# Five tiles of six with the gate in two products: channel 128 written into PSUM ahead of the cosine product

## The chip, the cores and the metric

The kernel runs on one core of one Trainium2 chip. The metric is the device time of one execution in microseconds, the median of the runs. PE is the matrix engine (TensorE), PEld its weight loads, DVE the vector engine, ACT the scalar engine, POOL GpSimd, SP the engine that only issues DMAs.

## The reference

Two parts follow each other: a Fourier mixing of x (8 batches of 3008 rows of 256 channels), and a gated feed-forward layer on the rows that come out of it.

```python
X = np.fft.fft(x, axis=1)
X = np.fft.fft(X, axis=2)
x = X.real.reshape(24064, 256)
gate = np.maximum(x @ w_gate, 0.0)      # w_gate, w_val: 256 x 1536
val = x @ w_val
out = gate * val @ w_out                # w_out: 1536 x 256
```

## The kernel before, in words

**Symmetry.** The real part of the two transforms is a cosine part minus a sine part over the channels. The transform over the channels is multiplied into the weights at the start (WA for the cosine part, WB for the sine part), so that the layer works on U and V, the sequence transforms of folded channels. Two output rows that mirror each other have the same cosine product and opposite sine products. One row set is U·WA + V·WB, the other U·WA - V·WB. V's row 0 would be empty and carries channel 128 instead, whose sign is not turned in the mirrored rows; so WM, the matrix that turns the first set into the second, is -2·WB with row 0 at zero.

**Tiles.** A tile is one slice of 128 hidden units (12 slices, `fi`) by one block of columns. Batch 0 has four blocks (`segments`, 376 or 377 columns), batches 1 to 7 have three (`thirds`, 504, 504 and 497 columns): 36 tiles a batch. A tile gives h for both row sets (`half_h`), in bf16, and 12 tiles of a block are then multiplied with w_out in `out_steps` while the next block's tiles are made.

**An old tile** makes six products: two into g (lines 541 and 542), ACT's relu into SBUF (556), then WM onto the same g (546) and a second relu; likewise two into v, the multiplication with the first relu on DVE (564), WM onto v, and the second multiplication.

**A split tile** (`pair_of_tiles`, 631) has the gate in two products in banks of their own: sine gq (637) and cosine gp (638). ACT copies gq to SBUF as q (641). The sum gp + q is DVE's (647), one input from PSUM. For the difference, ACT has written -2·b2·c for channel 128 into qm (`ch128_part`, 629; c is a row that all partitions hold, CB), POOL adds q (642), DVE subtracts qm from gp (657). Both signs then go through `relu_mult` (568), which reads the gate from SBUF and v from PSUM. v takes three products, as before.

**Order.** The schedule is by hand: every engine runs its instructions in the order in which the program makes them. Tiles go in pairs, one split and one old. Between their steps lie output products (`run(todo_out, ...)`, four at a time), steps of the next batch's DFT (`todo_dft`, numbers per pair in line 739), one eviction or sum at a time (`run_one`), and on POOL the folds and gathers for the batch after the next (`run_fold`, with a credit in us per pair, 2.2 in batch 1 and 1.75 after). The folds (`fold_steps`, 132) are made in batches 1 to 5 and read two SBUF inputs each; the gathers are indirect DMAs that POOL issues (95).

**PSUM** has eight banks: g and v two each (psG), o two (psO, output products), d0 and d1 one each (psD, the two halves of a DFT family, 379). The DFT's odd half is copied to SBUF by ACT (364), and DVE makes sum and difference with the even half from PSUM (367). SBUF scratch of 512 columns comes from `space()`, eight buffers.

Of the kernel before, what the change touches and what calls it, by code (L numbers as in the profile page):

```python
# [32 lines left out]
def kernel(  # L33
# [20 lines left out]
    psG = ctx.enter_context(tc.tile_pool(name="psG", bufs=2, space=PS))  # L54
# [13 lines left out]
    wr = [[single(f"wr{i}{c}", [128, 2, 512], BF16) for c in range(3)] for i in range(2)]  # L68
# [224 lines left out]
    for s in weights(0, (psG, "g", "v"), nc.scalar):  # L293
        s()
# [38 lines left out]
    hp = ctx.enter_context(tc.tile_pool(name="hp", bufs=2 * NF + 2, space=SB))  # L333
# [26 lines left out]
    def combine(st, dst, fam, p, now=True):  # L360
        n = NE if fam == 0 else NJ
        pe, po = st[1], st[0]
        es = rp.tile([128, NE], F32, name="es", tag="es", bufs=2)
        evict.insert(0, lambda: nc.scalar.copy(es[p, 0:n], pe[p, 0:n]))
        for d, op in zip(half_of(dst, fam), (ALU.add, ALU.subtract)):
            m = d.shape[-1]
            sums.append(lambda d=d, op=op, m=m: nc.vector.tensor_tensor(d[p], es[p, 0:m], po[p, 0:m], op=op))  # L367
        if now:
            flush()

    def family(b, dst, fam, sine, pool=None, tags=("d0", "d1")):

        n, cols = (NE, slice(0, NE)) if fam == 0 else (NJ, slice(NE, NK))
        src, tab = (GG[b % 2], tabS) if sine else (FF[b % 2], tabC)
        st = {}

        def mm(par, t, nyq=False):
            if par not in st:
                st[par] = (pool or psD).tile([128, 512], F32, name="d", tag=tags[par])
            rows = slice(0, ROWS[par][t])  # L380
            if nyq:
                nc.tensor.matmul(st[par][0:1, 0:n], lhsT=FF[b % 2][rows, fam, t, par, 128:129], rhs=tabC[rows, 2 * t + par, cols],
                                 start=False, stop=(t == 2), skip_group_check=True)
            else:
                nc.tensor.matmul(st[par][:, 0:n], lhsT=src[rows, 1 - fam if sine else fam, t, par, 0:128],  # L385
                                 rhs=tab[rows, 2 * t + par, cols], start=(t == 0), stop=(t == 2))
        return mm, lambda now=True: combine(st, dst, fam, slice(0, 128), now)

    def dft_first(U, V):

        parts = [(family(0, U, 1, False), 1), (family(0, V, 1, True, psO, ("o", "o")), 2)]
        for t in range(3):
            for (mm, fin), kinds in parts:
                for nyq in range(kinds):
                    for par in (1, 0):
                        mm(par, t, nyq)
                if t == 2:
                    fin()

    def dft_steps(b, U, V, fams, nyq=False, now=False):  # L400
        steps = []
        for fam in fams:
            for dst, sine in ((V, True), (U, False)):
                mm, fin = family(b, dst, fam, sine)
                part = [lambda par=par, t=t, mm=mm: mm(par, t) for par in (1, 0) for t in range(3)]
                if sine and nyq:
                    part.append(lambda mm=mm: [mm(par, t, True) for par in (1, 0) for t in range(3)])
                part[-1] = lambda last=part[-1], fin=fin: (last(), fin(now))
                steps += part
        return steps  # L410

    def nyquist_steps(g, N):

        def one(fam):
            n, cols = (NE, slice(0, NE)) if fam == 0 else (NJ, slice(NE, NK))
            if not paired:
                flush()
            d = psD.tile([128, 512], F32, name="d", tag="d1")
            for k in range(6):
                t, par = k // 2, k % 2  # L420
                rows = slice(0, ROWS[par][t])
                nc.tensor.matmul(d[0:4, 0:n], lhsT=FN[rows, fam, t, par, g].rearrange("p s b -> p (s b)"),  # L422
                                 rhs=tabC[rows, 2 * t + par, cols], start=(k == 0), stop=(k == 5))
            evict.insert(0, lambda: nc.scalar.copy(N[0:4, fam, 0:n], d[0:4, 0:n]))
        return [lambda: one(1), lambda: one(0)]
# [80 lines left out]
    def gate_128():  # L506
        p = psD.tile([128, 512], F32, name="d", tag="d0")
        for f in range(NF):
            nc.tensor.matmul(p[:, f:f + 1], lhsT=WB[0][0:1, f * 128:(f + 1) * 128], rhs=one[:], start=True, stop=True)
        nc.vector.tensor_scalar(b2[:], p[:, 0:NF], scalar1=-2.0, op0=ALU.mult, scalar2=None)  # L510
    more[(2, 2)] = [gate_128]

    DFT_0 = (0, 0, 0, 0, 3, 0, 0, 0, 4, 3, 3, 0), (0,) * 6 + (1,) * 6, (2, 3, 3, 3, 3, 3, 3, 0, 0, 0, 0, 0)
    todo_out, todo_dft, todo_fold = [], [], []
# [33 lines left out]
    def bank(tag):  # L548
        return psG.tile([128, 512], F32, name=tag, tag=tag)

    def space():
        return rp.tile([128, 512], F32, name="r", tag="r", bufs=8)
# [9 lines left out]
    def mult(st, sign):  # L562
        n = st["n"]
        nc.vector.tensor_tensor(half_h(st, sign), st["r"][:, 0:n], st["v"][:, 0:n], op=ALU.mult)  # L564

    def relu_mult(st, sign):
        n = st["n"]
        nc.vector.scalar_tensor_tensor(half_h(st, sign), in0=st["s"][sign][:, 0:n], scalar=0.0, in1=st["v"][:, 0:n],  # L568
# [10 lines left out]
    def gate(st):  # L579
        st["g"] = bank("g")  # L580
        two(st["g"], st, 0)
        relu(st)
# [10 lines left out]
    def single_tile(st, outs, extra=()):  # L593

        gate(st)
# [12 lines left out]
    def first_tile(st, extra):  # L608

        third = st["fi"] % 3 == 2  # L610
        st["g"] = psD.tile([128, 512], F32, name="d", tag="d1") if third else bank("g")
# [5 lines left out]
        st["v"] = psD.tile([128, 512], F32, name="d", tag="d0") if third else bank("v")  # L617
# [8 lines left out]
    def ch128_part(s):  # L626

        s["qm"] = space()
        nc.scalar.activation(s["qm"][:, 0:s["n"]], s["c"], ACTF.Copy, scale=b2[:, s["fi"]:s["fi"] + 1])  # L629

    def pair_of_tiles(s, st, outs, fold_us, ahead):
# [3 lines left out]
        n = s["n"]  # L635
        gq, gp = bank("g"), bank("g")
        nc.tensor.matmul(gq[:, 0:n], lhsT=WB[0][:, s["f"]], rhs=s["vs"], start=True, stop=True)  # L637
        nc.tensor.matmul(gp[:, 0:n], lhsT=WA[0][:, s["f"]], rhs=s["us"], start=True, stop=True)  # L638
        qm = s["qm"]
        q, sp = space(), space()  # L640
        nc.scalar.copy(q[:, 0:n], gq[:, 0:n])  # L641
        nc.gpsimd.tensor_tensor(qm[:, 0:n], qm[:, 0:n], q[:, 0:n], op=ALU.add)  # L642
        run_fold(fold_us)
        if pending is not None:
            finish(pending)
        s["s"] = (sp, qm)
        nc.vector.tensor_tensor(sp[:, 0:n], gp[:, 0:n], q[:, 0:n], op=ALU.add)  # L647
        run(todo_out, outs)
        gate(st)
        if ahead is not None:  # L650
            ch128_part(ahead)
        run_one(evict)
        value(st)
        mult(st, 0)
        run(todo_out, outs)
        value(s)
        nc.vector.tensor_tensor(qm[:, 0:n], gp[:, 0:n], qm[:, 0:n], op=ALU.subtract)  # L657
        relu_mult(s, 0)
        mirror(st["g"], st, 0)
        relu(st)  # L660
        run_one(evict)
        run(todo_out, outs)
        finish(st)
        run_one(sums)
        run(todo_out, outs)
        return s

    ahead = None

    for b in range(B):  # L670
# [4 lines left out]
        for blk, block in enumerate(blocks):  # L675
# [9 lines left out]
            if blk == (0 if b else 2) and b + 1 < B:  # L685
                Un, Vn = new_uv()
                todo_dft = dft_steps(b + 1, Un, Vn, (1, 0), now=not b)
                CBn = up.tile([128, 4 * NJ + 2], BF16, name="CB", tag="CB")
                steps, todo_dft = todo_dft, []
# [27 lines left out]
            elif not paired:  # L717
                for fi in range(NF):
                    st = tile_of(block, fi, (U, V, CB))
                    add_h(st, hs)  # L720
                    if (blk, fi) == (3, 11):
                        ahead = tile_of(thirds[0], 0, (Un, Vn, CBn))
                        more[(blk, fi)] = [lambda: ch128_part(ahead)]
                    pending = single_tile(st, per_tile // 2, more_b.get((blk, fi), ()))
                    run(todo_dft, DFT_0[blk - 1][fi])
            else:
                for fi in range(0, NF, 2):
                    at = 6 * blk + fi // 2
                    s, st = ahead, tile_of(block, fi + 1, (U, V, CB))
                    for tile_ in (s, st):  # L730
                        add_h(tile_, hs)
                    if fi + 2 < NF:
                        ahead = tile_of(block, fi + 2, (U, V, CB))
                    elif blk < 2:
                        ahead = tile_of(blocks[blk + 1], 0, (U, V, CB))
                    else:
                        ahead = tile_of(blocks[0], 0, (Un, Vn, CBn)) if b + 1 < B else None
                    pending = pair_of_tiles(s, st, per_tile // 2, 2.2 if b == 1 else 1.75, ahead)
                    run(todo_dft, (2, 1, 3)[at % 3] if at < 9 else (1, 1, 2, 1, 3)[at - 9] if at < 14 and b % 2 else (2, 1, 3, 0, 0)[at - 9] if at < 14 else 0)
# [39 lines left out]
```

## Time and profile before

| what | us |
|---|---|
| median of 3 runs | 670.19 (670.15 to 670.19) |
| the profiled execution | 670.19 |
| its span | 668.4 |
| PE busy | 645.5 |
| DVE busy | 564.9 |
| ACT busy | 426.5 |
| POOL busy | 404.0 |

The span is the time from the first to the last instruction in the profile; the execution's own time lies around it. A matmul's mean duration is longer than the distance to the next, since matmuls are pipelined: the chain of waits shows what each of them holds up. A row of a group shows the line, engine, operation, tiles and shapes, then the busy time and the mean of one, then the idle time of the engine just before these instructions with what ended it. In the timeline the columns are start, duration, engine, line and operation; a bracket gives the idle time before and who ended it.

### The profile page before, as it was taken

To read this page: it belongs to the slowest core of one execution; us is meant where nothing else is said; L and a number is where in the kernel's file an instruction comes from. 1 tells how busy PE (TensorE), PEld (TensorE's weight loads), DVE (VectorE), ACT (ScalarE), POOL (GpSimd) and SP (SyncE) were. 2 spreads that over 40 slices of the span, in tenths; PEclk is the share of its full clock that TensorE was granted. 3 is DMA by queue.
4 is the path that set the end of the run, shared out by engine and by line. 5 is a ranking of instruction groups with operands and counts; after the bars stand their busy time and mean duration, and the time that the engine had idled before them with its cause. 6 is when DMAs were issued, how large, how long until landed. Compare 5 with 4: busy or idle time off the path is not lost.

```text
span 668.4 us, 12335 instructions
## 1 busy us (share of the span) xinstructions
PE 645.5 (97%) x4266; PEld 413.6 (62%) x4266; DVE 564.9 (85%) x988; ACT 426.5 (64%) x798; POOL 404.0 (60%) x485
## 2 busy tenths in 40 slices
PE   0999999999999999999999999999999999999997
PEld 0456676665666666665666666666666666666666
DVE  8876566998988999898898989889898999999991
ACT  8796566666665666665666656656665666666662
POOL 7589996886777675775667657676622222233330
PEclk9999999999999999999999999999999999999999
DMA  8922653242324133142322422211121112111112
GB/s 223 196 65 63 193 154 111 71 132 62 102 77 123 47 104 86 38 139 64 89 76 54 133 86 78 78 31 34 46 71 31 42 38 70 33 52 42 46 48 78
DMA packets 42439, 55.26 MB, mean 83 GB/s; under 512 B 5153, under 2 KB 32353, under 8 KB 42376
## 3 DMA queue, kind: packets, MB, share of 16 engines
q1 hardware_dynamic: 34552, 39.23, 19.4%
q0 software_dynamic: 7536, 14.72, 9.1%
q8 instruction: 33, 0.54, 0.4%
q10 hardware_dynamic: 288, 0.52, 0.2%
q14 instruction: 30, 0.25, 0.1%
HBM read 32.14 MB, written 24.67 MB: 85 GB/s over the span
## 4 chain that ended last, share of the span: by engine, by line
PE 93%; DVE 4%; ACT 2%; issue 1%; DMA 0%; SPq 0%; POOL 0%; DVEq 0%; ACTq 0%; POOLq 0%
PE o L470 37%; PE v L546 9%; PE v L541 9%; PE v L542 9%; PE g L546 5%; PE g L541 5%; PE g L542 5%; PE d L385 4%; PE g L637 4%; PE g L638 4%; PE d L422 1%; ACT r L556 1%; DVE PQ L114 1%; DVE m L226 1%; DVE XG L106 1%
## 5 line engine op out<-in xcount | busy, mean ns | idle before, releaser
L470 PE MATMUL o<-wo,h 128*128 128x256 bf16 x2304 | 345.6, 273 | 0.0
L470 PEld LDWEIGHTS <-h 128*128 128x128 bf16 x2304 | 225.4, 98 | 123.9 <-issue 1.7
L642 POOL TENSOR_TENSOR r<-r 128x504 f32<-128x504 f32 (+1 forms) x126 | 157.6, 1250 | 227.3 <-ACT r L641 227.2
L556 ACT ACTIVATE r<-g 128x504 f32<-128x504 f32 (+3 forms) x340 | 191.2, 565 | 135.8 <-PE g L542 102.3
L564 DVE TENSOR_TENSOR h<-r,v 128x504 bf16<-128x504 f32 (+3 forms) x340 | 214.6, 640 | 53.1 <-ACT r L556 33.3
L568 DVE SCALAR_TENSOR_TENSOR h<-r,v 128x504 bf16<-128x504 f32 (+1 forms) x252 | 169.4, 672 | 27.6 <-PE v L546 23.7
L641 ACT COPY r<-g 128x504 f32<-128x504 f32 (+1 forms) x126 | 72.8, 578 | 82.8 <-PE g L637 82.8
L546 PE MATMUL v<-V,WM 128*128 128x504 bf16 (+3 forms) x296 | 108.6, 367 | 0.3
L541 PE MATMUL v<-U,WA 128*128 128x504 bf16 (+3 forms) x296 | 108.7, 367 | 0.1
L542 PE MATMUL v<-V,WB 128*128 128x504 bf16 (+3 forms) x296 | 108.7, 367 | 0.0
L629 ACT ACTIVATE r<-CB,b 128x504 f32<-128x504 bf16 (+1 forms) x126 | 88.8, 705 | 0.0
L647 DVE TENSOR_TENSOR r<-g,r 128x504 f32<-128x504 f32 (+1 forms) x126 | 84.9, 674 | 0.0
L657 DVE TENSOR_TENSOR r<-g,r 128x504 f32<-128x504 f32 (+1 forms) x126 | 84.9, 674 | 0.0
L546 PEld LDWEIGHTS <-WM 128*128 128x128 bf16 x474 | 46.2, 98 | 35.0 <-issue 0.5
L476 ACT COPY os<-o 128x512 f32<-128x512 f32 x96 | 55.8, 581 | 10.6 <-PE o L470 8.5
L541 PEld LDWEIGHTS <-WA 128*128 128x128 bf16 x474 | 46.3, 98 | 26.1 <-issue 3.5
L546 PE MATMUL g<-V,WM 128*128 128x504 bf16 (+3 forms) x170 | 61.4, 361 | 0.7 <-ACT r L556 0.5
L542 PE MATMUL g<-V,WB 128*128 128x504 bf16 (+3 forms) x170 | 61.4, 361 | 0.5 <-DVE V L367 0.5
L541 PE MATMUL g<-U,WA 128*128 128x504 bf16 (+3 forms) x170 | 61.5, 362 | 0.4 <-DVE U L367 0.3
L542 PEld LDWEIGHTS <-WB 128*128 128x128 bf16 x474 | 46.3, 98 | 23.7 <-ACT WB L284 0.7
L95 POOL DMA_INDIRECT XG<-in_x_dram,gidx x48 | 48.8, 1017 | 8.8 <-issue 5.4
L106 POOL TENSOR_TENSOR XG<-XG,XD 128x510 f32<-128x510 f32 x42 | 52.3, 1266 | 0.1
(108 smaller groups left out, 494.5 us busy)
## 6 DMA issues: line engine op xcount, KB each, us to landing
out_dram<-os SPq DMA_DIRECT2D x118, 128.0 KB
XD<-in_x_dram SPq DMA_DIRECT2D x30, 256.0 KB
out_dram<-os SPq DMA_DIRECT2D x62, 120.0 KB
XD<-in_x_dram SPq DMA_DIRECT2D x16, 240.0 KB
CB<-ch SPq DMA_DIRECT2D x7, 376.2 KB
out_dram<-os SPq DMA_DIRECT2D x10, 127.0 KB
XG<-in_x_dram,gidx POOLq DMA_INDIRECT x48, 3.9
wr<-in_moe_w_gate_dram POOLq DMA_DIRECT2D x3, 256.0 KB, 7.3
```

The source lines that it names most:

```text
L470: nc.tensor.matmul(st["p"][:, q, :], lhsT=hs[f][:, sign, h0:h0 + 128], rhs=wo[:, f, :], start=(f == 0), stop=(f == NF - 1))
L541: nc.tensor.matmul(bank[:, 0:st["n"]], lhsT=WA[i][:, st["f"]], rhs=st["us"], start=True, stop=False)
L542: nc.tensor.matmul(bank[:, 0:st["n"]], lhsT=WB[i][:, st["f"]], rhs=st["vs"], start=False, stop=True)
L546: nc.tensor.matmul(bank[:, 0:st["n"]], lhsT=WM[i][:, st["f"]], rhs=st["vs"], start=False, stop=True, skip_group_check=True)
L556: nc.scalar.activation(st["r"][:, 0:st["n"]], st["g"][:, 0:st["n"]], ACTF.Relu)
L564: nc.vector.tensor_tensor(half_h(st, sign), st["r"][:, 0:n], st["v"][:, 0:n], op=ALU.mult)
L568: nc.vector.scalar_tensor_tensor(half_h(st, sign), in0=st["s"][sign][:, 0:n], scalar=0.0, in1=st["v"][:, 0:n], op0=ALU.max, op1=ALU.mult)
L629: nc.scalar.activation(s["qm"][:, 0:s["n"]], s["c"], ACTF.Copy, scale=b2[:, s["fi"]:s["fi"] + 1])
L641: nc.scalar.copy(q[:, 0:n], gq[:, 0:n])
L642: nc.gpsimd.tensor_tensor(qm[:, 0:n], qm[:, 0:n], q[:, 0:n], op=ALU.add)
L647: nc.vector.tensor_tensor(sp[:, 0:n], gp[:, 0:n], q[:, 0:n], op=ALU.add)
L657: nc.vector.tensor_tensor(qm[:, 0:n], gp[:, 0:n], qm[:, 0:n], op=ALU.subtract)
```

## The change

Instead of pairs there is one loop over tiles, `slot(cur, nxt, after)`, with the kinds "nnnnno": five split tiles, then an old one. In a slot the gate of the next tile is made and the value of the current one.

For a split tile the steps are: `seed`, one slot ahead, in which ACT writes b2·c (now with the factor 1) into the PSUM bank of the cosine part; `sine_part`, one product into g, with WM, which holds no channel 128, copied by ACT to SBUF as q with the factor -0.5; `cosine_part`, one product onto the seeded bank, which ACT copies to SBUF, and POOL's difference copy - q; and `plus`, DVE's sum copy + q, both inputs from SBUF. An old tile's gate keeps its three products on g, all in the slot ahead of its value.

The PSUM banks are dealt out anew: g one, p (cosine part) two, v two, o two, d one. The DFT's halves therefore go one behind the other through d, with an eviction between them (`end(par)`), and the steps per slot are DFT_EVEN and DFT_ODD. `space()` has twelve buffers; the weights' raw tiles share the pool of h. The folds' credit is 1.1 per slot in batch 1 and 0.9 after. Batch 0 takes other banks for the same steps, and its last tile primes the two p banks with a product each and makes the first split gate.

```diff
-    psG = ctx.enter_context(tc.tile_pool(name="psG", bufs=2, space=PS))
+    psG = ctx.enter_context(tc.tile_pool(name="psG", bufs=1, space=PS))
+    psP = ctx.enter_context(tc.tile_pool(name="psP", bufs=2, space=PS))
+    psV = ctx.enter_context(tc.tile_pool(name="psV", bufs=2, space=PS))
...
-        nc.vector.tensor_scalar(b2[:], p[:, 0:NF], scalar1=-2.0, op0=ALU.mult, scalar2=None)
+        nc.vector.tensor_scalar(b2[:], p[:, 0:NF], scalar1=1.0, op0=ALU.mult, scalar2=None)
...
+    DFT_EVEN = (3, 0, 3, 0, 0, 0) * 4 + (0,) * 12
+    DFT_ODD = (3, 0, 3, 0, 0, 0) * 3 + (1, 0, 1, 0, 3, 0, 3) + (0,) * 11
...
-        return rp.tile([128, 512], F32, name="r", tag="r", bufs=8)
+        return rp.tile([128, 512], F32, name="r", tag="r", bufs=12)
...
+    KINDS = "nnnnno"
...
+    def prime():
+        p = bank("p")
+        nc.tensor.matmul(p[:], lhsT=WA[0][:, 0:128], rhs=U[:, 0:512], start=True, stop=True)
+        return p
+
+    def seed(st, p=None):
+        if st is None or st["kind"] == "o":
+            return
+        st["p"] = p or bank("p")
+        nc.scalar.activation(st["p"][:, 0:st["n"]], st["c"], ACTF.Copy, scale=b2[:, st["fi"]:st["fi"] + 1])
+
+    def sine_part(st):
+        n = st["n"]
+        st["g"] = bank("g")
+        nc.tensor.matmul(st["g"][:, 0:n], lhsT=WM[0][:, st["f"]], rhs=st["vs"], start=True, stop=True)
+        st["q"] = space()
+        nc.scalar.activation(st["q"][:, 0:n], st["g"][:, 0:n], ACTF.Copy, scale=-0.5)
+
+    def cosine_part(st):
+        n = st["n"]
+        nc.tensor.matmul(st["p"][:, 0:n], lhsT=WA[0][:, st["f"]], rhs=st["us"], start=False, stop=True, skip_group_check=True)
+        st["s"] = copy, sp, sm = [space() for _ in range(3)]
+        nc.scalar.copy(copy[:, 0:n], st["p"][:, 0:n])
+        nc.gpsimd.tensor_tensor(sm[:, 0:n], copy[:, 0:n], st["q"][:, 0:n], op=ALU.subtract)
+
+    def plus(st):
+        n, (copy, sp, _) = st["n"], st["s"]
+        nc.vector.tensor_tensor(sp[:, 0:n], copy[:, 0:n], st["q"][:, 0:n], op=ALU.add)
+
+    def slot(cur, nxt, after, outs, fold_us):
+        stop = len(todo_out)
+        def out(part):
+            run(todo_out, len(todo_out) - stop + outs * part // 8)
+        old = nxt is not None and nxt["kind"] == "o"
+        new = nxt is not None and not old
+        if old:
+            gate(nxt)
+        elif new and cur["kind"] != "o":
+            sine_part(nxt)
+        out(3)
+        if new:
+            if cur["kind"] == "o":
+                sine_part(nxt)
+                out(5)
+            cosine_part(nxt)
 +        run_fold(fold_us)
+        seed(after)
+        out(5)
+        finish(pending)
+        value(cur)
+        if cur["kind"] == "o":
+            mult(cur, 0, cur["first"])
+        else:
+            relu_mult(cur, 0)
+        if new:
+            plus(nxt)
+        run_one(evict)
+        run_one(sums)
+        out(6)
+        if old:
+            nxt["first"] = nxt["r"]
+            mirror(nxt["g"], nxt, 0)
+            relu(nxt)
+        out(8)
+        return cur
...
+                    pending = slot(cur, *ahead, per_tile, 1.1 if b == 1 else .9)
+                    run(todo_dft, DFT_ODD[at] if b % 2 else DFT_EVEN[at])
```

## The prediction

> **What bounds the kernel now.** I read the page's busy times first, then the busy times by stretch, with the span after the first batch cut into the seven equal parts that batches 1 to 7 take (the first product of line 637 starts at 111.2, the last batch's tiles end at 653.6: 77.5 us each).
>
> ```profile
> PE 645.5 (97%) x4266; PEld 413.6 (62%) x4266; DVE 564.9 (85%) x988; ACT 426.5 (64%) x798; POOL 404.0 (60%) x485
> ```
>
> ```profile
> 111.20:188.70 77.50, 77.36 (x499) 47.97 (x497) 68.78 (x116) 49.29 (x90) 59.21 (x67) 1.00 0.31 90
> 188.70:266.20 77.50, 77.50 (x515) 50.11 (x513) 69.94 (x118) 49.02 (x88) 53.59 (x62) 1.00 0.31 89
> 266.20:343.70 77.50, 77.50 (x509) 49.10 (x508) 68.16 (x114) 48.14 (x88) 51.20 (x60) 1.00 0.29 84
> 343.70:421.10 77.40, 77.40 (x514) 50.04 (x513) 69.83 (x117) 49.19 (x90) 52.72 (x62) 1.00 0.30 86
> 421.10:498.60 77.50, 77.50 (x511) 49.28 (x509) 68.16 (x114) 48.50 (x89) 46.49 (x56) 1.00 0.15 47
> 498.60:576.10 77.50, 77.50 (x513) 50.04 (x512) 70.09 (x117) 49.06 (x89) 22.50 (x18) 1.00 0.16 46
> ```
>
> Columns after the length: PE, weight loads, DVE, ACT, POOL, granted clock, DMA. The reader is to see that PE has no hole in these batches and the full clock, so every product taken away is time, as long as nothing else becomes late; and that POOL is a different engine in batches 1 to 4 (folds of later batches) than in 6 and 7. In the chain of waits a 504-column product takes 0.21 us (three in 0.635: 0.2115), four output products 0.44 (0.109 each). Twelve thirds of a batch are 36 tiles, so a tile lasts 2.15 us.
>
> **What goes from PE.** A batch has 18 split tiles (5 products) and 18 old ones (6); after it, 30 and 6. So 12 x 7 = 84 products go: 84 x 0.2115 = **-17.8 us**, 2.54 per batch. The DFT and output products stay.
>
> **What is added on each engine.** These are the prices that the page gives:
>
> ```profile
> L642 POOL TENSOR_TENSOR r<-r 128x504 f32<-128x504 f32 (+1 forms) x126 | 157.6, 1250 | 227.3 <-ACT r L641 227.2
> ...
> L641 ACT COPY r<-g 128x504 f32<-128x504 f32 (+1 forms) x126 | 72.8, 578 | 82.8 <-PE g L637 82.8
> ...
> L629 ACT ACTIVATE r<-CB,b 128x504 f32<-128x504 bf16 (+1 forms) x126 | 88.8, 705 | 0.0
> L647 DVE TENSOR_TENSOR r<-g,r 128x504 f32<-128x504 f32 (+1 forms) x126 | 84.9, 674 | 0.0
> ```
>
> and this stretch of the timeline gives what they take one behind the other:
>
> ```profile
> 303.47 0.71 ACT L629 ACTIVATE r<-CB,b 128x504 f32<-128x504 bf16 x1
> 303.58 1.09 POOL L114 TENSOR_TENSOR PQ<-XG 128x510 f32<-128x510 f32 x1
> ...
> 303.60 0.68 DVE L564 TENSOR_TENSOR h<-r,v 128x504 bf16<-128x504 f32 x1 [0.16 <-ACT r L556]
> ...
> 304.02 0.38 PE L546 MATMUL g<-V,WM 128*128 128x504 bf16 x1
> ...
> 304.20 0.68 DVE L657 TENSOR_TENSOR r<-g,r 128x504 f32<-128x504 f32 x1
> ...
> 304.43 0.59 ACT L556 ACTIVATE r<-g 128x504 f32<-128x504 f32 x1 [0.26 <-PE g L546]
> ```
>
> The reader is to see that DVE starts its next operation 0.60 after the last (a stretch later 0.59), not 0.68; ACT likewise 0.49 behind a read of PSUM (300.18 to 300.67) and 0.60 behind L629; and that a product's result is read 0.41 after its start (304.02 to 304.43).
>
> A slot of the changed loop with a split tile behind a split tile has 5 products and 8 output products on PE: 5 x 0.2115 + 8 x 0.109 = 1.93 us, plus its share of the DFT.
> - **DVE**: two relu-multiplies and the add `plus`, 3 x 0.59 = 1.77. The subtraction of L657 goes to POOL. Six slots (five split, one old) come to 5 x 1.77 + 2 x 0.59 + 0.6 for the DFT's sums = 10.6, against PE's 5 x 1.93 + 2.14 + 0.64 = 12.4: it fits.
> - **ACT**: two copies and the seed, 2 x 0.49 + 0.60 = 1.58, with evictions 1.8 of 1.93; six slots about 10.2 of 12.4. The seed writes PSUM from SBUF, which the trace doesn't show; its ends are the copy (0.578) and L629 (0.705); I take L629, the same operation, and the lower end would change nothing, since it is wanted by PE only in the next slot, 0.2 to 0.3 us after it ends.
> - **POOL**: 12 more subtractions per batch at 1.25 = +15.0. With the columns above: 74.2, 68.6, 66.2, 67.7, 61.5, then 37.5 and 38.7 of some 76 us. POOL's subtraction of a tile is wanted two slots later, about 2.5 us after it should be ready, which covers a fold in front of it (up to 1.82).
> - **The DFT** keeps its products; its one bank d is emptied by ACT (0.36) in the slot between the odd and the even half, and by two sums in the slots after, so nobody waits; were that cover gone, each of 8 halves would cost PE up to 0.9 us in a batch.
> - **SP** keeps its DMAs and their order; POOL's gathers stay behind the same fold steps, one tile at a time instead of two.
>
> **A new wait of PE.** psG now has one buffer for g. Of a slot whose next tile is old, the mirrored gate product is the last long one, then come 2 + 3 output products (0.545 us) and then the next tile's sine product, which needs that bank. The relu ends 0.41 + 0.59 after the mirror product's start, and PE takes up ACT's end 0.05 later (40.85 to 40.90 in the trace): 1.05 - 0.2115 - 0.545 = **0.29 us** of PE idle, with all outputs of the slot and the DFT queued behind it. Nothing covers it: the DFT steps lie in other slots (but for one). 42 old tiles x 0.29 = **+12.2 us**. Before, g had two buffers and the trace shows no such wait.
>
> **Start of batch 1**: two priming products (0.43) and a cosine product that waits for its seed (0.41 + 0.71 + 0.05 after the prime, with 0.64 of work before it: about 0.5): **+0.9**. It holds tile 11 of the last segment, once.
>
> **The step that decides: the add's two inputs.** L647 took one input from PSUM. `plus` takes both, the copy and q, from SBUF, 30 times per batch, while POOL's subtractions and folds read two SBUF inputs each. In a slot the copy ends at 1.53 us, POOL's subtraction runs from 1.67 to 2.9, and DVE reaches `plus` at 2.56: they meet in every slot. No row shows such a pair. While POOL folds, every DVE operation of batches 1 to 7 has one input in PSUM; the folds that DVE makes itself run while POOL only issues DMAs, and POOL then waits for them (L309, 7.2 us idle). So the ends are: nothing lost (an add of 510 elements with both inputs in SBUF, L114 on DVE, took 686 ns with POOL issuing DMAs), and full turns, 0.68 us of POOL per add. What is nearest to a meeting is this:
>
> ```profile
> 10.21 0.83 POOL L214 DMA_DIRECT2D wr<-in_moe_w_gate_dram  x1
> 10.60 0.49 DVE L222 TENSOR_SCALAR qd<-dvec,ums 128x129 f32<-128x129 f32 x1
> ...
> 11.66 0.29 DVE L222 TENSOR_SCALAR qd<-dvec,ums 128x129 f32<-128x129 f32 x1
> ```
>
> The same operation on the same shape took 0.49 and 0.29; the long one ended 0.05 behind POOL's instruction. It is one row and another kind of operation, but it is a sign of turns. I take turns, for the time in which the add passes data: 504 x 1.04 ns (L106 against L114 on DVE: 1216 - 686 over 510 elements) = 0.525. Per batch 30 x 0.525 = 15.8, less 3.0 for adds that meet a gather (some 9% of the time) and for POOL's operations overlapping by 0.03. POOL's column becomes 87.0, 81.4, 79.0, 80.5, 74.3. Where it is above PE's 77.5 - 2.54 + 6 x 0.29 = 76.7, DVE waits at `plus`, the relu-multiplies queue behind it, and PE waits for them at its mirror products. Batches 1 to 4: +9.5 + 3.9 + 1.5 + 3.0; batches 5 to 7: -0.8 each; start +0.9. Sum **+16.4**.
>
> The trace can show no more here. The Trainium skill, SBUF — State Buffer, Who interferes with whom, says it outright: a DVE instruction with two SBUF inputs and a GpSimd instruction that reads SBUF exclude each other, and the second to start waits for the whole of the first. It speaks against this change, and no run so far shows it; by it the forecast's sum stands nearer its upper end, by its absence the next case holds.
>
> The profiled execution took 670.19 us, its span 668.4, the rest lies around it; the median of the runs is the same 670.19. So 670.2 + 16.4 = **687 us**. With full turns and nothing taken off, the columns are 94.5, 88.9, 86.5, 88.0, 81.8, the sum +52 and the time 722; with 0.42 per add it is 675. Range of this case 674 to 712.
>
> **Rivals.**
> 1. *Faster: the add and POOL don't disturb each other.* For it: L114's 686 ns, and that six-slot sums of all engines fit. Then -17.8 + 12.2 + 0.9 = -4.7: **665.5** (655 if the wait for g is hidden after all). The point from which it turns: at about 0.34 us of POOL per add batch 1 alone eats the 4.7 us. That is half of the way between the ends, which is why neither case is far ahead.
> 2. *Slower without turns*: POOL in batch 1 has 1.1 us of folds per slot beside 1.25; five split slots take 2.35 each against PE's 2.0, so it falls back 1.7 us in six slots, over its 2.5 of slack with one long fold; and ACT has 0.2 us of slack at the seed. Each 0.04 us in 210 split slots is 8 us: **674**.
> 3. *It comes out even*: a small loss of either kind against the 4.7 us: **670**.
>
> **Chances**: turns 0.50 (687), rival 1 0.36 (665.5), rival 2 0.07, rival 3 0.07. Within 0.2% (1.3 us, about what a measurement of this kernel can tell from no change) is rival 3; slower is 0.57. The range for 8 in 10 must reach to rival 1: 662 to 710.
>
> **What would show it.** Of the changed kernel: 84 fewer 504-column products; PE idle of about 0.3 us before the sine product, released by the relu, 41 times; `plus` at more than 0.68 us, or POOL's subtraction above 1.25 in the slots where both run, in all batches; batches 1 to 4 longer than 77.5 and 6 to 7 about 76.7. If `plus` stays at 0.68 and POOL's rows at 1.25, the decisive step is wrong and the time is rival 1's. If batches 6 and 7 are long as well, another engine than POOL is late.

## The result and the profile after

The changed kernel takes **743.55 us** (median of 4 runs, 742.31 to 744.28) against 670.19: ratio 1.109 [1.107, 1.111], 73 us slower. The forecast was 687, its range ended at 710. The profiled execution took 742.31 us, its span 740.5 (before: 670.19 and 668.4).

The page of the changed kernel, busy times, granted clock and chain of waits by engine:

```profile
PE 655.8 (89%) x4182; PEld 408.7 (55%) x4184; DVE 640.9 (87%) x946; ACT 532.4 (72%) x1008; POOL 550.9 (74%) x569
...
PEclk9999998879999999999989999999999999999999
...
PE 60%; DVE 21%; issue 14%; ACT 3%; POOL 1%; DMA 0%; DVEq 0%; SPq 0%; ACTq 0%; POOLq 0%
```

84 products are gone, and still PE's busy time grew by 10.3 us. Part of that is the clock: in the columns by batch below, PE's busy time times what the granted clock lacked comes to some 15 us in batches 1 to 4. Another part is bookkeeping, since a product with a pause behind it shows its full 0.38 us where the next one used to follow after 0.21. PE is no longer what is always busy. DVE's busy time grew by 76 us (564.9 before), though it makes fewer instructions (946 for 988), and it has 21% of the chain. No engine has its whole span full; that is what a loop of waits between engines looks like.

The costliest groups of the changed kernel (busy, mean ns of one, then idle time before them and who ended it):

```profile
L679 POOL TENSOR_TENSOR r<-r 128x504 f32<-128x504 f32 (+1 forms) x210 | 274.4, 1310 | 150.9 <-ACT r L678 144.7
...
L582 DVE SCALAR_TENSOR_TENSOR h<-r,v 128x504 bf16<-128x504 f32 (+1 forms) x420 | 268.3, 670 | 47.6 <-PE v L560 41.9
L683 DVE TENSOR_TENSOR r<-r 128x504 f32<-128x504 f32 (+1 forms) x210 | 249.0, 1185 | 2.1 <-ACT r L678 2.1
...
L560 PE MATMUL v<-V,WM 128*128 128x504 bf16 (+3 forms) x296 | 110.3, 373 | 55.9 <-DVE h L582 52.9
L665 ACT ACTIVATE p<-CB,b 128x504 f32<-128x504 bf16 (+1 forms) x210 | 145.0, 691 | 0.6 <-PE v L556 0.6
...
L113 POOL TENSOR_TENSOR XG<-XG,XD 128x510 f32<-128x510 f32 x42 | 60.9, 1463 | 0.1
```

Read the second and third numbers. The relu-multiply (L582) has the mean that it had, 670. The add `plus` (L683) has a mean of 1185 where L647 had 674: 210 x 0.51 = 107 us of DVE's time. POOL's fold L113 went from 1266 ns (L106 of before) to 1463. PE stood idle for 55.9 us ahead of its mirror product (L560), and 52.9 of that was ended by the relu-multiply, which stands behind the add on DVE. The seed (L665), a write into PSUM, costs 691 ns, and PE hardly waited for ACT.

All adds in the view of one source line (shortest, median, longest ns):

```profile
L683 DVE TENSOR_TENSOR r<-r x210: 665/874/8695, 113.7 to 721.5; 128x504 f32<-128x504 f32 x70, 128x497 f32<-128x497 f32 x35
```

An undisturbed add still takes 665 ns; half take over 874, and one takes 8695. Thirteen took over 1.9 us and have 43 of the 107 us; three of these (2.30 to 2.33 us) waited for one long fold of 1.8 us, the other ten for two to seven POOL instructions, and those ten have 38 us.

Busy times by batch, 1 to 6, cut at the first sine product of each (the columns of the forecast's table):

```profile
111.40:216.90 105.50, 83.21 (x483) 48.63 (x482) 95.20 (x109) 65.03 (x121) 81.74 (x79) 0.90 0.23 68
216.90:307.10 90.20, 79.56 (x499) 49.23 (x499) 84.22 (x108) 64.40 (x118) 76.41 (x73) 0.98 0.25 73
307.10:398.80 91.70, 82.13 (x511) 50.16 (x511) 82.55 (x111) 64.93 (x120) 76.02 (x74) 0.96 0.24 73
398.80:488.60 89.80, 79.30 (x498) 49.08 (x498) 84.26 (x111) 64.19 (x118) 76.22 (x74) 0.98 0.25 74
488.60:574.10 85.50, 79.55 (x511) 49.30 (x511) 78.64 (x113) 64.78 (x120) 70.48 (x69) 1.00 0.15 46
574.10:650.60 76.50, 75.74 (x498) 48.66 (x498) 69.59 (x110) 63.98 (x118) 37.66 (x30) 1.00 0.15 47
```

Cut in the same way, the batches of before took 77.7, 77.2, 79.5, 77.2, 79.5, 77.2 and 88.7 with the end (odd batches hold the Nyquist products). So the 72 us are +27.9, +13.0, +12.2, +12.7, +6.0, -0.7, +1.2: they lie in the batches with folds on POOL, and batch 6, where POOL only subtracts, is faster than before. And POOL, the last busy column, is idle for 13.8 us of batch 2.

One add that meets one subtraction, in the timeline of batch 3 (start, duration):

```profile
328.77 1.25 POOL L679 TENSOR_TENSOR r<-r 128x504 f32<-128x504 f32 x1
...
329.29 1.28 DVE L683 TENSOR_TENSOR r<-r 128x504 f32<-128x504 f32 x1
...
329.99 1.71 POOL L113 TENSOR_TENSOR XG<-XG,XD 128x510 f32<-128x510 f32 x1
```

POOL's subtraction ends at 330.02, the add at 330.57, 0.55 later; POOL's fold, taken up at 329.99, ends 1.13 behind the add, a little less than its undisturbed length of 1.27. That is a turn: the add waits for all of the subtraction, then the fold waits for the add. The rule weighed in the forecast (the Trainium skill, SBUF — State Buffer, Who interferes with whom: of the two the second waits for the whole of the first) agrees with these three numbers.

The longest add, in batch 1:

```profile
139.88 1.27 POOL L679 TENSOR_TENSOR r<-r 128x504 f32<-128x504 f32 x1
...
140.28 8.70 DVE L683 TENSOR_TENSOR r<-r 128x504 f32<-128x504 f32 x1
...
141.10 1.28 POOL L113 TENSOR_TENSOR XG<-XG,XD 128x510 f32<-128x510 f32 x1
...
142.32 1.25 POOL L679 TENSOR_TENSOR r<-r 128x504 f32<-128x504 f32 x1
...
143.53 2.48 POOL L113 TENSOR_TENSOR XG<-XG,XD 128x510 f32<-128x510 f32 x2
...
145.97 1.24 POOL L679 TENSOR_TENSOR r<-r 128x504 f32<-128x504 f32 x1
147.18 1.25 POOL L113 TENSOR_TENSOR XG<-XG,XD 128x510 f32<-128x510 f32 x1
...
150.66 0.58 PE L560 MATMUL v<-V,WM 128*128 128x504 bf16 x1 [7.76 <-DVE h L582]
```

Here the turn is missed. Seven POOL instructions run one behind the other at their plain lengths, the next taken up as the last ends, and the add ends at 148.98, 0.55 behind the seventh (148.43). PE waits 7.76 us and comes back at a lower clock (its product then takes 0.58 in place of 0.38).

### The profile page after: what moved, and what is told of

It reads as the page before. It is cut to its first block, busy times and chain, and to the rows that moved or that the text cites. A ratio compares the mean times of both kernels' runs of the same rounds, so it can differ in the third digit from the quotient of the medians.

```text
span 740.5 us, 12781 instructions
## 1 busy us (share of the span) xinstructions
PE 655.8 (89%) x4182; PEld 408.7 (55%) x4184; DVE 640.9 (87%) x946; ACT 532.4 (72%) x1008; POOL 550.9 (74%) x569
## 4 chain that ended last, share of the span: by engine, by line
PE 60%; DVE 21%; issue 14%; ACT 3%; POOL 1%; DMA 0%; DVEq 0%; SPq 0%; ACTq 0%; POOLq 0%
PE o L481 22%; DVE h L582 10%; PE v L560 7%; DVE r L683 6%; PE v L556 6%; PE v L555 6%; PE g L670 5%; PE p L676 4%; PE d L383 2%; ACT r L570 2%; DVE h L578 1%; PE d L433 1%; PE g L560 1%; PE p L560 1%; PE p L556 1%
## 5 line engine op out<-in xcount | busy, mean ns | idle before, releaser
L679 POOL TENSOR_TENSOR r<-r 128x504 f32<-128x504 f32 (+1 forms) x210 | 274.4, 1310 | 150.9 <-ACT r L678 144.7
L582 DVE SCALAR_TENSOR_TENSOR h<-r,v 128x504 bf16<-128x504 f32 (+1 forms) x420 | 268.3, 670 | 47.6 <-PE v L560 41.9
L683 DVE TENSOR_TENSOR r<-r 128x504 f32<-128x504 f32 (+1 forms) x210 | 249.0, 1185 | 2.1 <-ACT r L678 2.1
L672 ACT ACTIVATE r<-g 128x504 f32<-128x504 f32 (+1 forms) x210 | 124.1, 591 | 89.1 <-PE g L670 54.2
L560 PE MATMUL v<-V,WM 128*128 128x504 bf16 (+3 forms) x296 | 110.3, 373 | 55.9 <-DVE h L582 52.9
L665 ACT ACTIVATE p<-CB,b 128x504 f32<-128x504 bf16 (+1 forms) x210 | 145.0, 691 | 0.6 <-PE v L556 0.6
L578 DVE TENSOR_TENSOR h<-r,v 128x376 bf16<-128x376 f32 (+3 forms) x172 | 101.0, 605 | 28.3 <-PE v L560 16.9
L678 ACT COPY r<-p 128x504 f32<-128x504 f32 (+1 forms) x210 | 121.5, 579 | 1.5 <-PE p L676 1.1
L570 ACT ACTIVATE r<-g 128x504 f32<-128x504 f32 (+3 forms) x94 | 54.7, 582 | 73.2 <-PE g L560 40.1
L670 PE MATMUL g<-V,WM 128*128 128x504 bf16 (+1 forms) x210 | 80.2, 382 | 4.8 <-ACT r L672 0.2
L676 PE MATMUL p<-U,WA 128*128 128x504 bf16 (+1 forms) x210 | 79.7, 380 | 0.5 <-ACT p L665 0.4
L102 POOL DMA_INDIRECT XG<-in_x_dram,gidx x48 | 56.3, 1172 | 8.7 <-issue 5.7
L113 POOL TENSOR_TENSOR XG<-XG,XD 128x510 f32<-128x510 f32 x42 | 60.9, 1463 | 0.1
```

The costliest lines, as they stand in the source:

```text
L560: nc.tensor.matmul(bank[:, 0:st["n"]], lhsT=WM[i][:, st["f"]], rhs=st["vs"], start=False, stop=True, skip_group_check=True)
L570: nc.scalar.activation(st["r"][:, 0:st["n"]], st["g"][:, 0:st["n"]], ACTF.Relu)
L665: nc.scalar.activation(st["p"][:, 0:st["n"]], st["c"], ACTF.Copy, scale=b2[:, st["fi"]:st["fi"] + 1])
L670: nc.tensor.matmul(st["g"][:, 0:n], lhsT=WM[0][:, st["f"]], rhs=st["vs"], start=True, stop=True)
L672: nc.scalar.activation(st["q"][:, 0:n], st["g"][:, 0:n], ACTF.Copy, scale=-0.5)
L678: nc.scalar.copy(copy[:, 0:n], st["p"][:, 0:n])
```

## The experiments

The theories. **Turns on DVE**: an add with both inputs in SBUF waits for POOL instructions that read SBUF, and what it loses is lost on DVE, where the relu-multiplies stand behind it. Rival A, **POOL's column** (the forecast's own reckoning): the loss counts as POOL's time, so it shows only where POOL is nearly full. Rival B: most of the 73 us is from the new order and the banks, not from the add.

### e1: the sum takes the cosine part from PSUM

```
-        nc.vector.tensor_tensor(sp[:, 0:n], copy[:, 0:n], st["q"][:, 0:n], op=ALU.add)
+        nc.vector.tensor_tensor(sp[:, 0:n], st["p"][:, 0:n], st["q"][:, 0:n], op=ALU.add)
```

> The changed kernel, but the add takes the cosine part from PSUM instead of ScalarE's copy: one input in SBUF, everything else as it is. If the add and POOL take turns because both inputs come from SBUF: the add 0.68 us everywhere (median 0.87, longest 8.7 now), POOL's subtraction 1.25, batches 1 to 5 at 76 to 79 us, time 663 to 669. If POOL's own load (68 to 74 us of work in a batch of 77) or another engine is what is late: adds still wait or others do, and the time stays above 715.

Measured: **670.54 us**, ratio to before 1.0006 [0.9997, 1.0016]. All 73 us are gone; the time is 1.5 us above the range expected for it. The page's busy times and the source line of the add in this kernel:

```profile
PE 637.0 (95%) x4184; PEld 405.0 (61%) x4184; DVE 541.2 (81%) x946; ACT 529.4 (79%) x1008; POOL 507.6 (76%) x569
```

```profile
L683 DVE TENSOR_TENSOR r<-p,r x210: 668/676/683, 114.1 to 649.7; 128x504 f32<-128x504 f32 x70, 128x497 f32<-128x497 f32 x35
```

The same 210 adds now lie between 668 and 683 ns, beside the same subtractions and folds. Against it the changed kernel's DVE is busy 99.7 us longer and POOL 43.3. Rival B falls: every other part of the change is in this kernel. That the sum now waits for the cosine product itself and no longer for ACT's copy doesn't explain the gain, since DVE stood idle for that copy for only 2.1 us in the changed kernel (row L683 above). But e1 is not faster than before, as rival 1 of the forecast had it (665.5): its batches take 79.6, 76.5, 79.0, 76.5, 79.0, 76.5 and 90.1. The even ones gain the 0.7 to 0.8 forecast; batch 1 loses 1.9, and the last with the end 1.4.

This also sizes the loss. By batch the adds of the changed kernel have 30.6, 21.3, 17.0, 19.2, 11.4, 3.9 and 3.9 us over 0.675 each; its batches are longer than those of this kernel by 26.0, 13.7, 12.7, 13.4, 6.5, 0.0 and -0.2. What DVE loses above some 4 to 8 us in a batch is lost to the kernel, although e1's DVE is idle for 10 to 15 us of a batch.

### e2: no folds for batches 3 to 7

```
+        if b > 2:
+            steps = [s if s in gathers or s[0] == 0.0 else (s[0], lambda: None) for s in steps]
```

> The changed kernel without POOL's fold arithmetic for batches 3 to 7 (gathers and loads stay, so the rows of those batches are wrong). If what costs is the meeting of the add with a chain of POOL operations: batches 1 to 5 become like batch 6 (76.5; odd ones 78), adds at 0.67 to 1.04, time 664 to 670. If each meeting costs by itself, with the subtraction alone as well: batches 1 to 5 stay above 82 and the time above 700.

Measured, in one run: **687.46 us**. Folds carry 56 of the 73 us; neither expectation held. The batches take 87.2, 79.7, 81.3, 80.2, 79.0, 76.5. Batch 1 still makes what is left of batch 2's folds, and there are adds like this one, behind a gather (timeline, batch 3; lines are two higher here):

```profile
271.45 1.25 POOL L102 DMA_INDIRECT XG<-in_x_dram,gidx  x1 [0.17 <-issue]
...
272.74 2.44 POOL L681 TENSOR_TENSOR r<-r 128x497 f32<-128x497 f32 x2
272.90 2.81 DVE L685 TENSOR_TENSOR r<-r 128x497 f32<-128x497 f32 x1
```

The gather held up one subtraction, so two run in a row, and the add ends behind both. So what this add lost went by how many reading instructions POOL had in a row when it came; batches 6 and 7, where POOL only subtracts, are as in the changed kernel.

### e5: the kernel before, with only its sum's inputs both in SBUF

```
+        cp = rp.tile([128, 512], F32, name="cp", tag="cp", bufs=1)
+        nc.scalar.copy(cp[:, 0:n], gp[:, 0:n])
...
-        nc.vector.tensor_tensor(sp[:, 0:n], gp[:, 0:n], q[:, 0:n], op=ALU.add)
+        nc.vector.tensor_tensor(sp[:, 0:n], cp[:, 0:n], q[:, 0:n], op=ALU.add)
```

> The kernel before with one thing of the change alone: ScalarE also copies the cosine part to SBUF (126 copies more), and DVE's sum takes both inputs from SBUF. If only POOL's column counts, as the prediction summed it: columns of 69, 63, 61, 62 and 56 us, all below 77.5, and no loss: 670 to 673. If DVE's wait at each meeting counts: DVE is busy 69 of 77.5 and 18 waits of 0.5 us or more a batch do not fit, so batches 1 to 5 grow by 3 us or more: above 685.

Measured: **705.56 us**, ratio 1.0523 [1.0505, 1.0541]. The source line of this sum:

```profile
L649 DVE TENSOR_TENSOR r<-cp,r x126: 892/1352/3647, 113.0 to 686.4; 128x504 f32<-128x504 f32 x84, 128x497 f32<-128x497 f32 x42
```

Not one of 126 sums is below 892 ns (669 to 678 before). The added copies aren't what they wait for: ahead of these sums DVE was idle for ACT's copy once, for 0.2 us. The batches take 87.7, 82.3, 86.0, 84.1, 82.3, 79.8 and 91.3. This settles A: POOL has but 434.8 us of work in a span of 704.7, so its column is far from full, and batch 6, in which POOL was busy for 22.5 of 77.5 us, grows too, by 2.6. Eighteen adds of this form per batch, with their copies, cost the kernel before 35 us, in another order of work and without any other part of the change.

### e7 and e8: what POOL does while the add runs

Both are e2 with POOL's subtraction replaced, so no fold is in the way after batch 1.

e7:

```
-        nc.gpsimd.tensor_tensor(sm[:, 0:n], copy[:, 0:n], st["q"][:, 0:n], op=ALU.subtract)
+        nc.gpsimd.memset(sm[:, 0:n], 0.0)
```

e8:

```
-        nc.gpsimd.tensor_tensor(sm[:, 0:n], copy[:, 0:n], st["q"][:, 0:n], op=ALU.subtract)
+        nc.gpsimd.tensor_copy(sm[:, 0:n], copy[:, 0:n])
```

> As the kernel without the fold arithmetic (687.5), and POOL's subtraction is replaced by writing zeros of the same size (the difference and the folds of batches 3 to 7 are left out, so half of the rows are wrong). If the add and POOL share a way of reading: adds 0.67 to 0.70 even while POOL writes, time 664 to 671. If any POOL instruction holds the add: it is still stretched where the two meet, and the time stays above 680.

> The same, but POOL copies the cosine part instead of subtracting (one input from SBUF; the difference and the folds are left out). If two inputs on both sides are needed for a turn: adds 0.68 and 664 to 671. If one POOL read is enough: adds stretched to as much as the copy's rest plus 0.54, fewer and shorter than with the subtraction, 668 to 682.

Measured, one run each: e7 **668.24 us**, e8 **668.97**. The source lines of e7's add and of its memset, and one meeting in its timeline:

```profile
L685 DVE TENSOR_TENSOR r<-r x210: 669/675/1510, 113.7 to 647.4; 128x504 f32<-128x504 f32 x70, 128x497 f32<-128x497 f32 x35
```

```profile
L681 POOL MEMSET r<- x210: 513/517/521, 108.9 to 643.8; 128x504 f32 x70, 128x497 f32 x35
```

```profile
128.71 0.68 DVE L685 TENSOR_TENSOR r<-r 128x504 f32<-128x504 f32 x1
128.91 0.52 POOL L681 MEMSET r<- 128x504 f32 x1
```

In 125 of the 210 adds of e7 a memset runs for over 0.15 us beside the add, and none of these adds is above 0.72 us; the memset keeps its 0.517. The one of 1510 met a leftover fold. A POOL instruction that only writes SBUF doesn't hold the add, nor does the add hold it. The Trainium skill, SBUF — State Buffer, Who interferes with whom, says so too, and this run agrees. The add of e7 reads two SBUF inputs like that of the changed kernel, so the two inputs alone, without POOL reading beside them, cost nothing.

e8 says less: its time lies in both expected ranges, and the copy of 0.6 us mostly ends before the add comes. In batch 1 six copies began while an add had still 0.4 us or more to go, and all six took 0.87 to 1.12 us where the median is 0.607; the first two began 0.03 us behind the start of an add of 0.683 and ended 0.46 behind its end. So a POOL instruction with one SBUF input waits for the add too; that such a copy holds an add, no case shows cleanly.

### e9: POOL waits for the sum before it folds

```
-        run_fold(fold_us)
...
             plus(nxt)
+            nc.gpsimd.tensor_copy(go[:, 1:2], nxt["s"][1][:, 0:1])
+        run_fold(fold_us)
```

> The changed kernel (sum of two SBUF inputs, all folds), but POOL gets its folds behind the add of the slot, and before them copies one column of the sum, so that it can't start a fold until the add has run. If part of the loss is turns that the add loses to several POOL operations in a row (adds of 2.3 to 8.7 us, some 30 us in all): no add above 1.9, time 705 to 730. If the plain turns are the whole loss: 740 to 750, or more for the added wait.

Measured: **732.95 us**, ratio 1.0932 [1.0913, 1.0950], between the two expectations. The adds in this kernel:

```profile
L683 DVE TENSOR_TENSOR r<-r x210: 665/960/4545, 113.7 to 712.5; 128x504 f32<-128x504 f32 x70, 128x497 f32<-128x497 f32 x35
```

Batch 1 fell from 105.6 to 92.2, the others stayed within 3 us (92.4, 88.8, 89.7, 87.0, 77.4, and 92.9 with the end). The longest wait is halved, the median is up: POOL is later, makes 210 small reads more, and in batches 6 and 7 all 30 adds are above 0.72 us in place of 24 and 21. The expectation of no add above 1.9 us failed: batch 1 has four of them in place of five, batches 2 to 5 ten in place of eight. So e9 made the missed turns of batch 1 shorter and took none away elsewhere. That waits for single POOL instructions cost time by themselves is seen in batch 5 of the changed kernel: no add there took over 1.9 us, and it lost 6.0.

### e4 and e6: the bank for g, with the sum from PSUM

e4 is e1 with six outputs instead of three ahead of the sine product in an old tile's slot; e6 is e4 with the seed of the tile after moved ahead of that sine product.

e4 against e1:

```
-        out(3)
+        out(6 if cur["kind"] == "o" else 3)
```

e6 against e4:

```
             if cur["kind"] == "o":
+                seed(after)
                 sine_part(nxt)
...
-        seed(after)
+        if not (new and cur["kind"] == "o"):
+            seed(after)
```

> As the first kernel of this call, and in a slot whose current tile is old six output products instead of three stand ahead of the next tile's sine product. If PE waits 0.29 us for the bank g at each of 42 old tiles and three outputs (0.33 us) cover it: 12 us less than the first kernel, 651 to 657. If something else sets the slots' length: within 3 us of the first kernel.

> The add from PSUM, six outputs ahead of the sine product behind an old tile, and in that slot the seed of the tile after is written before the sine product's copy instead of behind both copies. In the last such kernel PE no longer waited 0.29 us for the bank g but then for the seed (39 times). If ScalarE's order (second relu, q, copy, seed) is what made that wait, the seed now fills ScalarE's idle 0.55 us behind the relu, both waits go, 41 x 0.29 = 12 us: 657 to 661. If ScalarE's sum of work sets the slot: no less than 668.

Measured: e4 **672.6 us**, 1.0037 [1.0024, 1.0049]; e6 **659.93 us**, 0.9846 [0.9829, 0.9862]. First the wait itself, in the timeline of the changed kernel (batch 6):

```profile
599.21 0.38 PE L560 MATMUL g<-V,WM 128*128 128x504 bf16 x1
...
599.42 0.71 PE L481 MATMUL o<-wo,h 128*128 128x256 bf16 x5
599.62 0.59 ACT L570 ACTIVATE r<-g 128x504 f32<-128x504 f32 x1 [0.29 <-PE g L560]
...
600.26 0.37 PE L670 MATMUL g<-V,WM 128*128 128x504 bf16 x1
```

From the mirror product to the sine product it is 1.05; the product and five outputs hold 0.2115 + 0.545 of it, so 0.29 is lost. Then e4's timeline at the same place:

```profile
604.14 1.04 PE L481 MATMUL o<-wo,h 128*128 128x256 bf16 x8
...
605.01 0.38 PE L670 MATMUL g<-V,WM 128*128 128x504 bf16 x1
...
605.49 0.59 ACT L672 ACTIVATE r<-g 128x504 f32<-128x504 f32 x1 [0.55 <-PE g L670]
...
606.43 0.70 ACT L665 ACTIVATE p<-CB,b 128x504 f32<-128x504 bf16 x1
...
606.51 0.49 PE L481 MATMUL o<-wo,h 128*128 128x256 bf16 x3
...
607.18 0.37 PE L676 MATMUL p<-U,WA 128*128 128x504 bf16 x1 [0.19 <-ACT p L665]
```

The sine product follows the eight outputs at once (604.14 + 8 x 0.109 = 605.01), so the wait is gone; but ACT now gets its first copy later, and with it the seed, and in the next slot the cosine product waits for the seed. PE's three outputs before it began at 606.51 and hold 0.33, so from 606.84 to 607.18 PE loses 0.34: 0.05 more than the wait that went, and if all 42 places are like this one, 42 x 0.05 = 2.1 is just what e4 is slower than e1. The wait had only been passed on. In e6 ACT makes the seed ahead of that first copy, where it had stood idle for 0.55, and batch 2 has no hole on PE:

```profile
190.70:265.40 74.70, 74.70 (x501) 48.73 (x499) 65.96 (x110) 64.47 (x119) 68.94 (x76) 1.00 0.32 92
```

74.7 is 77.2 less 2.5: the 12 x 0.2115 = 2.54 of a batch, whole. e6 beats both kernels, by 10.3 us against before.

### e10 and e11: what is next in e6

e10 against e6:

```
-    KINDS = "nnnnno"
+    KINDS = "n"
```

e11 against e6:

```
-                    pending = slot(cur, *ahead, per_tile, 1.1 if b == 1 else .9)
+                    pending = slot(cur, *ahead, per_tile, .9)
```

> The best kernel so far (659.9: add from PSUM, early seed) with all tiles split instead of five of six. PE loses 42 more products, 8.9 us. If PE still sets the slots: 650 to 653. If POOL (36 subtractions of 1.25 and 30 us of folds: 75 of some 74 us) or DVE (1.77 and its sums in slots of 1.93, with no old tile to catch up in) sets them: batches 2 to 4 no shorter than 74.7, and 657 to 675.

> The best kernel so far with 0.9 us of folds per slot in batch 1 too, instead of 1.1. Batch 1 lasts 79.3 there, 1.8 more than batches 3 and 5, and PE waits 2.1 us at mirror products. If POOL's fuller slots in batch 1 make that: 658 to 659. If the start of the new loop makes it: within 0.5 of 659.9, or more where folds left over at the end of batch 1 hold up the next.

Measured: e10 **665.74 us**, 0.9936 [0.9919, 0.9952]; e11 **669.46**, 0.9987 [0.9977, 0.9996]. Batches 2 and 6 of e10, the same columns:

```profile
192.40:269.90 77.50, 75.25 (x494) 47.99 (x492) 69.03 (x116) 67.52 (x125) 76.04 (x81) 1.00 0.29 87
501.00:576.20 75.20, 74.68 (x494) 48.07 (x493) 69.45 (x117) 67.65 (x125) 45.15 (x37) 1.00 0.15 47
```

With all tiles split POOL is busy for 76.0 of the 77.5 us of batch 2, and the batch is 2.9 us longer than in e6: another 1.25 us on POOL for each old tile is more than the batch has. Batches 1 and 2 have 4.6 of the 5.8 us by which e10 is above e6. But POOL isn't all of it. Batch 6, where POOL is busy for only 45.2 of 75.2 us, is 0.5 us longer than in e6, with six products fewer: at eight mirror products there PE loses 1.7 us in sum until DVE's relu-multiply ends. These stand in slots in which DVE makes a DFT sum besides its other three operations and has no hole, with no old tile to catch up in.

In e11 the folds come later. PE's Nyquist product, still in batch 1, waits for POOL, and early in batch 2 the folds left over from batch 1 stand ahead of two subtractions for which DVE waits (two timelines):

```profile
157.23 1.28 PE L433 MATMUL d<-tabC,FN 128*4 128x376 bf16 x6 [4.04 <-POOL FN L151]
```

```profile
206.67 1.27 DVE L582 SCALAR_TENSOR_TENSOR h<-r,v 128x504 bf16<-128x504 f32 x2 [4.64 <-POOL r L679]
```

So the larger credit in batch 1 is needed, and what e6's batch 1 still loses (79.3, where 77.7 less 2.54 would be 75.2) is not had back by spreading the folds.

## Why the prediction was wrong

The case that was put first, slower by turns, is the one that came; it was priced at 16.4 us and cost 73.

- **PE's products**: right. 4266 less 84 is 4182, and e6 shows their price: 2.5 us in each of batches 2, 4 and 6.
- **The wait for g**: right, 0.29 us in the timeline; taken away in e6, batch 2 of e1 (76.5) falls by 1.8, against 6 x 0.29 = 1.74.
- **ACT, the seed**: taken as 0.705, measured 0.691; in the changed kernel PE waits for it 0.4 us in all. That the seed becomes late when ACT's order moves (e4) wasn't seen.
- **The start of batch 1**: forecast +0.9; the first sine product comes 0.2 us later than the first product of line 637 did (0.6 in e1). e1's batch 1 is then 1.9 longer than before and its last batch with the end 1.4, where the forecast without turns had -0.8 for each. These 4.9 us were not traced to a cause; of the 3.3 us of PE's idle time in that batch 1, 1.4 lie ahead of mirror products.
- **The step that decides, the add's inputs**: right that they take turns, that `plus` is above 0.68 and folds above 1.25, that batches 1 to 4 carry it (66 of 72 us), that 6 comes to 76.7 (76.5); 7 with the end was to be 0.8 shorter and is 1.2 longer. The one row for it, the 0.49 beside 0.29 of L222, had the right sign by luck: it is a TENSOR_SCALAR, whose row shows one input of 129 columns, beside a DMA that POOL issued, and in the changed kernel POOL's gathers alone stretched none of seven adds.
- **The failed step is the term of the turns**, where the prediction says "per batch 30 x 0.525 = 15.8, less 3.0" and puts it on "POOL's column", so that a batch is the longer of POOL's column and PE's path. Three things are wrong in it. First, **whose time it is**: it was counted as POOL's, as if POOL were packed and DVE had room. DVE pays 107 us, POOL 43, and POOL is idle for 13.8 us of batch 2, where its column left it no idle time: a late add holds the relu-multiplies, these hold PE's mirror products, PE's cosine product comes late, so ACT's copy, and POOL waits for the copy (144.7 us by its group's row). e1 has 66.5 us of DVE in batch 2's 76.5; 66.5 + 21.3 of lost time is 87.8 and the batch takes 90.2, while POOL's column said 81.4. This sum for DVE is no full reckoning either: batches 1, 3 and 5 take some 8 to 10 us more than it gives, which stays open. Second, **the size**: an add waits for what is left of POOL's instruction, not for its own 0.525. In batches 2 to 4 that is a mean of 0.64 per add, in batch 1 1.02. Third, **missed turns**: ten adds that waited for two to seven POOL instructions have 38 of the 107 us, 21 of them in batch 1. The prediction had a fixed order of turns. The clock, 0.90 in batch 1 with PE at rest for up to 7.8 us at a time, may add to this, and no run separates it; it isn't the cause, since batch 5 lost its 6.0 us at a granted clock of 1.00.
- By batch the term gave +9.5, +3.9, +1.5, +3.0, -0.8 for batches 1 to 5; measured were +27.9, +13.0, +12.2, +12.7, +6.0. Batch 5 tells most: POOL's column of 74.3 was below PE's 76.7, and still it lost 6.
- **The rivals**: rival 1 needed adds that aren't disturbed, and e1 makes it nearly so: 670.5 in place of 665.5. Rival 2's falling back of POOL in batch 1 can be at most the 2.7 us by which e1's batch 1 misses the forecast.
- **The range** ended at 710, and the result lies above even the 722 that was put for "full turns and nothing taken off". Both were taken on POOL's column; no bound had DVE as the one that waits.

## What to carry to other kernels

Before an operation of DVE gets two SBUF inputs, look for POOL instructions that read SBUF beside it; one input left in PSUM saved all 73 us here, for an edit of one word. Price such a wait on the engine that stands still and by what is queued behind it there, not on the engine that is in the way, and take the remaining length of the other's instructions in a row, not the own length. When a wait for a bank is filled with other work, check which engine's order that work delays (e4), and move what that engine can do in its idle time (e6).

## What the hardware showed

- A waiting DVE instruction counts as busy: the add's 8.70 us stand in DVE's busy time, so the busy shares don't tell waiting from work; only the source line's shortest, median and longest do.
- The add ends some 0.55 us behind the POOL instruction that it waited for (330.02 and 330.57; 148.43 and 148.98), less than its own 0.675. In the changed kernel this holds for every one of the 155 adds above 0.72 us: each ends 0.52 to 0.55 us behind the end of a reading POOL instruction.
- Turns aren't fair: POOL instructions that follow each other without a gap can pass the waiting add, seven in one case, while in batch 3 the very next fold had to wait. Of the adds of the changed kernel that had a further reading POOL instruction right behind the first, 73 came before it and ten were passed; all ten ended where POOL's reading instructions broke off, nine ahead of a gather and one ahead of 6.5 us of idle time. Nor has the first to start always the turn, as the Trainium skill (SBUF — State Buffer, Who interferes with whom: the order of issue decides) has it, if the start in the trace stands for the issue. In batch 1 of the changed kernel an add began 0.36 us ahead of a subtraction, beside a gather, and ended behind four of POOL's instructions (timeline):

```profile
182.25 1.04 POOL L102 DMA_INDIRECT XG<-in_x_dram,gidx  x1
...
182.94 6.28 DVE L683 TENSOR_TENSOR r<-r 128x497 f32<-128x497 f32 x1
183.30 2.44 POOL L679 TENSOR_TENSOR r<-r 128x497 f32<-128x497 f32 x2
185.69 1.81 POOL L128 TENSOR_TENSOR F<-PQ 128x768 bf16<-128x768 f32 x1
187.45 1.23 POOL L679 TENSOR_TENSOR r<-r 128x497 f32<-128x497 f32 x1
```

  What decides between a turn and a missed one stays open.
- A gather alone (L102, an indirect DMA) doesn't hold the add: in the changed kernel seven adds had only a gather beside them, and they took 665 to 678 ns. POOL's memset doesn't either (e7, 125 meetings, none above 0.72 us).
- A ScalarE write into PSUM took 691 ns (mean), the same function from SBUF to SBUF 705: no dearer.
